# A joint matmul for a group's maxima and the preceding group's sums, and other last loads of w_down, in a decode step of sliding attention beside a gated layer

## The chip, the cores and the metric

The kernel runs on one core of one Trainium2 chip. The metric is device time in microseconds of one launch; a time "of the runs" is the median of several executions. The profile shows one further execution, with its own time. TensorE is the matrix engine (PE in the profile; PEld is its loading of the stationary operand), VectorE is DVE, ScalarE is ACT, GpSimd is POOL, and SyncE (SP) issues nearly all the DMAs.

## The reference

One decode token for B = 2 rows of D = 512. The token is normalised and goes through two parallel branches, whose results are added to it:

```python
xn = _layernorm(x, axis=-1)
# branch A: 32 heads of 128, the last W = 2048 of 8192 cached positions
q = (xn @ wq) as (B, 32, 1, 128)
k, v = k_cache[:, :, Sk - W:, :], v_cache[:, :, Sk - W:, :]
scores = einsum("bhqd,bhkd->bhqk", q, k) * 128 ** -0.5
o = einsum("bhqk,bhkd->bhqd", softmax(scores), v) @ wo
# branch B: F = 1376
h = (xn @ w_gate) * (xn @ w_up)
out = x + o + h @ w_down
```

All is float32. The two caches' windows, wq, wo and the three matrices of branch B are 159 MB, each byte used once.

## The kernel before

**Layout.** All inputs but two small ones lie in one stream in DRAM, in the order in which they are wanted. Of the 128 partitions, 64 hold row b = 0 and 64 hold b = 1. The key window of a head is a tile of 128 x 4096: 32 positions of 128 elements on each partition. The 32 heads form 8 groups of HG = 4, so a group has N = 8 pairs of head and row.

**Loads.** `loads()` (lines 36 to 98) is a plan written out by hand: steps 0 to 24, each one DMA into one of three large buffers (`step0` to `step2`, 128 x 13824) or into the smaller `extra`. A step holds some key tiles `k`, value tiles `v`, and small pieces: four pieces of `wq` for each group, 32 pieces of `wo` (one for each head) and ten pieces of `w_down` (`wd`), each of the last two 128 x 512, which is 256 KB. Step 24 is several loads, each a DMA of its own: v(31), then wd(3, 4, 5), wd(6, 7), wd(8, 9). `issue` puts the loads on SP's queue in this order; a load waits until the old content of its buffer is no longer used.

**Order of the work.** Each engine runs its instructions in the order in which the program names them; `Program.emit` adds a wait where an instruction needs another engine's result. For each step from 3 to 20 (line 510): TensorE weighs the value tiles that have come (`weigh`: 8 matmuls for each head onto a bank of `o_ps`), projects later queries (`project`), multiplies w_down pieces that have come (`down`, onto `acc`); VectorE forms for each key tile the products with the query and their sums (`products`, `sums`, two passes over 128 x 4096). After the fourth head of a group comes `weights(g)` (line 364): VectorE takes the maxima over the free axis, transposes them, reduces again, spreads the result over the columns of `dg` with `mask`, TensorE multiplies the block matrix `halves` with `dg` so that all partitions of a row have the maxima of that row's four heads, VectorE reduces the two columns of each head to `nm` and subtracts it, and ScalarE takes the exponentials, in two halves. The first key tile after that carries `denominators(g)` (line 385): VectorE sums the exponentials over the free axis into `rs`, TensorE multiplies `ones` with `rs` to add up over the partitions; `reciprocals(g)` follows on VectorE. When the fourth value tile of a group has been weighed, `fold` copies the bank to SBUF on ScalarE, `gather` (four matmuls) picks the rows that belong together, `scaled` multiplies with the reciprocals on VectorE and `wo` multiplies the result with a piece of wo onto `acc`, a 2 x 512 accumulator.

**The end** (lines 557 to 590), with g = 7 and its heads 28 to 31: weigh(27) and the fold of group 6, denominators and reciprocals of group 7, gather and scaling of group 6, four wo matmuls onto `acc`, then weigh(28), the accumulator brought into `acc_g`, weigh(29), weigh(30), a fold, gather and scaling of three heads, their wo matmuls, weigh(31), its fold, and the pieces 3 to 9 of w_down around the gather, the scaling and the wo of the last head. In this last stretch the matmuls go onto `acc_g`, which has the 512 output columns as four groups of 128 columns at partitions 0, 32, 64 and 96 (`add_groups`, four matmuls of 128 columns), not onto `acc` (`add_rows`, one matmul of 512 columns). An f32 matmul shows as two passes in the profile.

In the profile nearly all instructions have line 197, which is the helper that emits them; they are told apart by their tiles.

Of the kernel before, what the change touches and what calls it, by code (L numbers as in the profile page):

```python
# [5 lines left out]
ALU = mybir.AluOpType  # L6
AX = mybir.AxisListType
# [3 lines left out]
P = 128  # L11
B, D, H, DH, SK, F = 2, 512, 32, 128, 8192, 1376
W = min(4096, max(256, SK // 4))
HB = P // B
J = W // HB
JG = J // 4
NC = D // P
FB = 4 * P
NFB = -(-F // FB)
# [4 lines left out]
HG = 4  # L24
NG = H // HG
GROUPS = [list(range(g * HG, g * HG + HG)) for g in range(NG)]
N = B * HG
M = 4 * N
CK, CO = J * DH, D
CX = B * NC + 4 * N + 2 * HG + 2 * NFB + 2  # L30
BUFS = 3
WIDTH = 13824
WIDTH_X = 4096
# [2 lines left out]
def loads():  # L36


    def units(kind, *ids):
        w = {"k": CK, "v": CK, "wo": CO, "wd": CO, "wq": HG * DH}[kind]  # L40
        return [(kind, i, w) for i in ids]

    def wq(g, *cs):
        return units("wq", *[(g, c) for c in cs])

    big = {
        1: units("k", 0, 1, 2),
        3: units("k", 3, 4) + units("v", 0),
        4: units("k", 5, 6) + units("v", 1),
        5: units("k", 7, 8) + units("v", 2),  # L50
    }
    k, v = 9, 3
    for n in range(6, 20):
        i = 1 + n % 2
        big[n] = units("k", *range(k, k + i)) + units("v", *range(v, v + 3 - i))
        k, v = k + i, v + 3 - i
    big[20] = units("k", 30, 31) + units("v", 24)
    big[21] = units("v", 25, 26, 27)
    big[22] = units("v", 28, 29)
    small = {  # L60
        1: wq(1, 0, 1, 2),
        3: wq(1, 3) + wq(2, 0, 1),
        4: wq(2, 2, 3) + units("wd", 0),
        5: wq(3, 0, 1, 2),
        6: units("wo", 0, 1, 2),
        7: wq(3, 3) + units("wo", 3) + wq(4, 0),
        8: units("wo", 4, 5, 6),
        9: units("wo", 7) + wq(4, 1, 2),
        10: wq(4, 3) + wq(5, 0, 1),
        11: units("wo", 8, 9, 10),  # L70
        12: units("wo", 11) + wq(5, 2, 3),
        13: wq(6, 0, 1, 2),
        14: units("wo", 12, 13, 14),
        15: units("wo", 15) + wq(6, 3) + wq(7, 0),
        16: units("wo", 16, 17, 18),
        17: units("wo", 19) + wq(7, 1, 2),
        18: wq(7, 3) + units("wd", 1, 2),
        19: units("wo", 20, 21, 22),
        20: units("wo", 23, 24, 25),
        21: units("wo", 26, 27, 28),  # L80
        22: units("wo", 29, 30, 31),
    }
    out = [
        (0, "x", [("c", 0, CX)] + wq(0, 0, 1, 2, 3)),
        (1, 0, big[1] + small[1]),
        (2, 1, [(w, 0, NC * F) for w in ("wg", "wu")]),
        (3, 2, big[3] + small[3]),
    ]
    for n in range(4, 23):
        out += [(n, (1, 0, 2)[(n - 4) % 3], big[n] + small[n])]  # L90
    out += [
        (23, "x", units("v", 30)),
        (24, 0, units("v", 31)),
        (24, 0, units("wd", 3, 4, 5)),
        (24, 0, units("wd", 6, 7)),
        (24, 0, units("wd", 8, 9)),
    ]
    return out
# [136 lines left out]
def build(nc, stream, x_nat, wd_rest, out):  # L235
    pr = Program(nc)
    pe, dve, act, pool = pr.pe, pr.dve, pr.act, pr.pool
# [5 lines left out]
    ones = pr.sb("ones", [P, P])  # L243
# [4 lines left out]
    xc = pr.sb("xc", [P, B, NC])  # L248
    sq = pr.sb("sq", [P, B, NC])
    xn = pr.sb("xn", [P, NC, B])  # L250
    halves = pr.sb("halves", [P, P])
    xnb = pr.sb("xnb", [P, NC, P])
    cst = pr.sb("cst", [P, CX])
    p_all = pr.sb("p", [P, 2, HG, JG, M])
# [1 line left out]
    mt = pr.sb("mt", [P, 32])  # L256
    mtt = pr.sb("mtt", [P, 32])
    mc = pr.sb("mc", [P, 1])
    dg = pr.sb("dg", [P, HG, 2])
    nm = pr.sb("nm", [P, HG])  # L260
    rs = pr.sb("rs", [P, N])
    rec = [pr.sb(f"rec{i}", [P, N]) for i in range(2)]
    oT = [pr.sb(f"oT{i}", [P, N]) for i in range(2)]
    o_sb = [pr.sb(f"o_sb{i}", [P, FB]) for i in range(2)]
# [8 lines left out]
    tr = pr.ps("tr", [P, FB])  # L273
# [28 lines left out]
    dve.memset(zero, 0.0)  # L302
    dve.memset(ones, 1.0)
    dve.memset(mt, 0.0)
    dve.memset(halves, 0.0)
    for b in range(B):
        dve.memset(halves[b * HB : (b + 1) * HB, b * HB : (b + 1) * HB], 1.0)
    for t in gu_ps:
        dve.memset(t, 0.0)
    pool.memset(p_all, 0.0)  # L310
# [1 line left out]
    c0 = got["c", 0]  # L312
    dve.tensor_copy(cst, c0)
    cut = [0]
    for w in (B * NC, 4 * N, 2 * HG, 2 * NFB, 2):
        cut.append(cut[-1] + w)
    xT = cst[:, cut[0] : cut[1]].rearrange("p (b c) -> p b c", b=B)
    pick = cst[:, cut[1] : cut[2]].rearrange("p (r n) -> p r n", r=4)
    mask = cst[:, cut[2] : cut[3]].rearrange("p (n q) -> p n q", q=2)
    sel = cst[:, cut[3] : cut[4]]  # L320
    id2 = cst[:B, cut[4] : cut[5]]

# [37 lines left out]
    def own(ap, counts):  # L360
        steps = (JG * M + 4 * B, 4, M, 1) if len(counts) == 4 else (JG * M + 4 * B, M, 1)
        return bass.AP(ap.tensor, ap.offset, [ap.ap[0]] + [list(t) for t in zip(steps, counts)])

    def weights(g):
        t = s_t[g % 2]
        dve.tensor_reduce(mt[:, 0:HG], t, axis=AX.X, op=ALU.max)
        dve.transpose(mtt, mt)
        dve.tensor_reduce(mc, mtt, axis=AX.X, op=ALU.max)
        dve.tensor_scalar(dg, mask, mc, None, ALU.mult)
        pe.matmul(tr[:, 0 : 2 * HG], halves, dg, start=True, stop=True)  # L370
        dve.tensor_reduce(
            nm, tr[:, 0 : 2 * HG].rearrange("p (n q) -> p n q", q=2), axis=AX.X, op=ALU.max
        )
        dve.tensor_tensor(
            t, t, nm.unsqueeze(2).to_broadcast([P, HG, J]), op=ALU.subtract
        )
        for b in range(B):
            half = slice(b * HB, (b + 1) * HB)
            act.activation(
                own(p_all[half, g % 2, 0, 0, 4 * b : 4 * b + 4], (HG, JG, 4)),  # L380
                t[half].rearrange("p h (i r) -> p h i r", r=4),
                AF.Exp, bias=zero[half], scale=SCALE,
            )

    def denominators(g):
        dve.tensor_reduce(
            rs, own(p_all[:, g % 2, 0, 0, 0:4], (HG, B, JG, 4)), axis=AX.XY, op=ALU.add
        )
        pe.matmul(tr[:, 0:N], ones, rs, start=True, stop=True)

    def reciprocals(g):
        dve.reciprocal(rec[g % 2], tr[:, 0:N])

    def weigh(h, bank=None, first=None, last=None):
        g, hh = divmod(h, HG)
# [22 lines left out]
    def scaled(g, lo=0, hi=N):  # L418
        dve.tensor_tensor(
            oT[g % 2][:, lo:hi], pk_ps[:, lo:hi], rec[g % 2][:, lo:hi], op=ALU.mult  # L420
        )
# [63 lines left out]
    def has(n, kind):  # L485
        return [i for k, i, _ in plan.get(n, []) if k == kind]
# [17 lines left out]
    open_q, open_g, late_wo = [], None, []  # L504
# [5 lines left out]
    for n in range(3, 21):  # L510
        ks, vs = has(n, "k"), has(n, "v")
        for h in late_wo:
            wo(h, add_rows)
        late_wo = []
        full = None
        for h in vs:
            if n > 3:
                weigh(h)
            if h % HG == HG - 1:
                full = h // HG  # L520
                fold(full)
        open_q += [(n, i) for i in has(n, "wq")]
        projections(ks[0] - 1)
        for c in has(n, "wd"):
            down(c, add_rows)
        if full is not None:
            gather(full)
        for x, h in enumerate(ks):
            products(h)
            if open_g is not None:  # L530
                denominators(open_g)
            if n == 3 and x == 0:
                turn()
            projections(h)
            sums(h)
            if open_g is not None:
                reciprocals(open_g)
                open_g = None
            if n == 20 and x == 1:
                weigh(25)  # L540
                weigh(26)
            if h % HG == HG - 1:
                weights(h // HG)
                open_g = h // HG
            if x == 0 and full is not None:
                scaled(full)
                for i in range(full * HG, full * HG + HG):
                    if i in has(n, "wo") or i in has(n - 1, "wo"):
                        wo(i, add_rows)
                    else:  # L550
                        late_wo.append(i)
        if n == 3:
            weigh(vs[0])
        if n < 20:
            issue(min([n] + [m - 1 for m, _ in open_q]) + 3 + (n == 19))

    g = NG - 1
    a, b, c, d = GROUPS[g]
    weigh(a - 1)
    fold(g - 1)  # L560
    denominators(g)
    reciprocals(g)
    gather(g - 1)
    scaled(g - 1)
    for h in GROUPS[g - 1]:
        wo(h, add_rows, last=(h == a - 1))
    issue(99)
# [9 lines left out]
        wo(h, add_groups)  # L577
    weigh(d, bank=0, first=True)
    fold(0)
    for i in range(3, 6):  # L580
        down(i, add_groups)
    gather(0, N - B, N)
    scaled(g, N - B, N)
# [10 lines left out]
def laid_out(x):  # L594
# [3 lines left out]
    a = x["A_x"].reshape(B, D)  # L598
    xs = np.zeros((P, CX), a.dtype)
    xs[:, : B * NC] = a.reshape(B, P, NC).transpose(1, 0, 2).reshape(P, B * NC)  # L600
    o = B * NC
# [3 lines left out]
    o += 4 * N  # L605
    for n in range(HG):
        for q in range(4):
            xs[32 * q + n, o + 2 * n + q % 2] = 1.0
    o += 2 * HG
    for n in range(NFB):  # L610
        for b in range(B):
            xs[32 * n + b, o + n * B + b] = 1.0
# [8 lines left out]
    wo = x["A_wo"].reshape(H, P, D)  # L621
# [4 lines left out]
    wd = x["B_w_down"]  # L626
# [47 lines left out]
```

## Time and profile before

| | us |
|---|---|
| median of 3 runs | 379.8 (379.56 to 380.12) |
| profiled execution | 377.47 |
| its span, first to last instruction | 376.0 |
| VectorE busy | 300.4 |
| TensorE busy | 202.7 |
| ScalarE busy | 15.1 |

The mean granted clock of TensorE is 0.709 of full speed. The profile is that of one execution, whose own time lies 2.3 us under the median of the runs. A group of instructions shows as: engine, operation, out<-in, shapes, count, busy time and mean time of one, and the idle time of the engine just before them with what ended it. The DMA rows give for each shape of load the time from issue to landing, which includes the time it stood in the queue.

### The profile page before, as it was taken

Reading aid. Unit: us, or ns where it says so; the run is one execution under the profiler, and the core shown is the slowest. Engines: PE = TensorE matmul, PEld = TensorE weight load, DVE = VectorE, ACT = ScalarE, POOL = GpSimd, SP = SyncE. Lnnn points to the kernel's source line nnn. Section 1 sums busy time; section 2 is a strip of 40 time slices with the busy share of each in tenths; the row PEclk is TensorE's granted clock in tenths of the full one; section 3 lists DMA queues with packets and bytes.
Section 4 is the critical chain, followed back from the end, with each engine's and each line's share of the span. In section 5 each row is a group of like instructions: output and inputs, shape, how many; then the busy total and the mean of one; then the engine's idle time right before and its main releaser. Section 6 shows DMA issues by size and latency. Waiting matters only on the chain.

```text
span 376.0 us, 2053 instructions
## 1 busy us (share of the span) xinstructions
PE 202.7 (54%) x900; PEld 62.3 (17%) x900; DVE 300.4 (80%) x159; ACT 15.1 (4%) x29; POOL 2.0 (1%) x5
## 2 busy tenths in 40 slices
PE   1552846814574457716457183580665274640996
PEld 1210121200220112101011021110121011200324
DVE  3059979999999997899499499959969995999500
ACT  1000100000000000000100000000000001000101
POOL 2000000000000000000000000000000000000000
PEclk9966856665666856859667756676588585575899
DMA  8999899898998999989999899999999999999995
GB/s 324 471 394 488 376 471 471 372 471 383 465 465 382 461 394 459 465 388 459 394 455 465 388 459 400 453 461 394 453 412 441 465 390 453 423 429 419 440 408 226
DMA packets 4300, 159.67 MB, mean 425 GB/s; under 512 B 482, under 2 KB 610, under 8 KB 1092
## 3 DMA queue, kind: packets, MB, share of 16 engines
q1 hardware_dynamic: 4176, 159.35, 98.4%
q10 hardware_dynamic: 116, 0.20, 0.1%
q8 instruction: 7, 0.11, 0.1%
q14 instruction: 1, 0.01, 0.0%
HBM read 159.48 MB, written 0.07 MB: 424 GB/s over the span
## 4 chain that ended last, share of the span: by engine, by line
DMA 50%; DVE 39%; PE 9%; ACT 0%; issue 0%; SPq 0%
DMA step<-in_stream_dram 50%; DVE s L197 19%; DVE step L197 19%; PE o_ps L197 4%; PE acc L197 3%; PE gu L197 1%; PE q L197 1%; ACT o_sb L197 0%; PE tr L197 0%; SPq L197 0%; DVE rs L197 0%; DVE mt L197 0%; DVE dg L197 0%; DVE mtt L197 0%; DVE mc L197 0%
## 5 line engine op out<-in xcount | busy, mean ns | idle before, releaser
L197 DVE TENSOR_TENSOR step<-step,q 128x4096 f32<-128x4096 f32 x32 | 141.1, 4410 | 41.3 <-DMA step<-in_stream_dram 41.3
L197 DVE TENSOR_REDUCE s<-step 128x32 f32<-128x4096 f32 x32 | 141.4, 4418 | 0.8
L197 PE MATMUL o_ps<-step,p 128*32 128x512 f32 x496 | 90.4, 830 | 60.8 <-DMA step<-in_stream_dram 60.7
L197 PE MATMUL q<-step,xnb 128*128 128x512 f32 x56 | 39.0, 831 | 26.8 <-DVE step L197 19.2
L197 PE MATMUL acc<-step,oT 128*2 128x512 f32 x56 | 38.7, 848 | 26.7 <-DVE oT L197 21.7
L197 PEld LDWEIGHTS o_ps<-step,p 128*32 128x32 f32 x496 | 19.5, 142 | 113.4 <-DMA step<-in_stream_dram 65.4
L197 PEld LDWEIGHTS q<-step,xnb 128*128 128x128 f32 x56 | 12.8, 256 | 51.4 <-DVE step L197 24.8
L197 ACT ACTIVATE p<-s,zero 64x128 f32<-64x128 f32 x16 | 6.4, 399 | 261.5 <-DVE s L197 261.4
L197 PE MATMUL gu<-step,xn 128*2 128x512 f32 (+1 forms) x48 | 9.6, 721 | 7.9 <-DMA step<-in_stream_dram 7.9
L197 PEld LDWEIGHTS acc<-step,oT 128*2 128x2 f32 x56 | 5.0, 102 | 52.9 <-DVE oT L197 22.4
L197 PE MATMUL gu<-cst,o_sb 128*128 128x8 f32 (+2 forms) x72 | 10.3, 270 | 3.9 <-ACT o_sb L197 3.8
L197 PE MATMUL tr<-rs,ones 128*128 128x8 f32 x16 | 3.9, 314 | 15.8 <-DVE rs L197 15.7
L197 PEld LDWEIGHTS gu<-cst,o_sb 128*128 128x128 f32 x72 | 9.5, 206 | 12.3 <-ACT o_sb L197 10.4
L197 DVE TENSOR_TENSOR oT<-gu,rec 128x8 f32<-128x8 f32 (+2 forms) x9 | 1.3, 140 | 12.2 <-PE gu L197 12.2
L197 PE MATMUL tr<-dg,halves 128*128 128x8 f32 x16 | 3.5, 293 | 13.7 <-DVE dg L197 13.7
L197 ACT COPY o_sb<-o_ps 128x512 f32<-128x512 f32 x9 | 5.3, 585 | 54.9 <-PE o_ps L197 54.9
L197 PEld LDWEIGHTS tr<-dg,halves 128*128 128x128 f32 x16 | 2.8, 218 | 22.9 <-DVE dg L197 22.1
L197 PE MATMUL q<-extra,xnb 128*128 128x512 f32 x8 | 5.6, 860 | 1.2 <-DVE xnb L197 1.2
L197 PEld LDWEIGHTS tr<-rs,ones 128*128 128x128 f32 x16 | 3.3, 254 | 16.9 <-DVE rs L197 16.9
L197 DVE TENSOR_REDUCE nm<-tr 128x4 f32<-128x8 f32 x8 | 1.3, 167 | 5.7 <-PE tr L197 5.7
L197 PE MATMUL tr<-st,mean_w 128*128 128x2 f32 x4 | 1.2, 363 | 7.4 <-DVE st L197 7.4
L197 PEld LDWEIGHTS gu<-step,xn 128*2 128x2 f32 x48 | 2.2, 100 | 15.6 <-DMA step<-in_stream_dram 9.1
(50 smaller groups left out, 45.8 us busy)
## 6 DMA issues: line engine op xcount, KB each, us to landing
step<-in_stream_dram SPq DMA_DIRECT2D x20, 6912.0 KB, 31.3
step<-in_stream_dram SPq DMA_DIRECT2D x1, 5504.0 KB, 34.0
step<-in_stream_dram SPq DMA_DIRECT2D x1, 4864.0 KB, 26.1
extra<-in_stream_dram SPq DMA_DIRECT2D x1, 2048.0 KB, 30.7
step<-in_stream_dram SPq DMA_DIRECT2D x1, 2048.0 KB, 27.2
extra<-in_stream_dram SPq DMA_DIRECT2D x1, 1052.0 KB, 5.5
step<-in_stream_dram SPq DMA_DIRECT2D x2, 512.0 KB, 21.5
step<-in_stream_dram SPq DMA_DIRECT2D x1, 768.0 KB, 20.3
```

The costliest lines, as they stand in the source:

```text
L197: ins = getattr(e, method)(*args, **kw)
```

## The change

- `weights(g)`: the matrix `halves` is gone. `mask` and `dg` have four columns for each head instead of two, one for each quarter of the partitions; `dg` and `rs` are two parts of one tile `both` (16 and 8 columns), and one matmul of `ones` with `both` spreads the maxima of group g and adds up the sums of group g - 1. The maxima of a row are then taken from the two columns of that row, with one reduction for each half of the partitions.
- `denominators(g)` forms `rs` alone, without a matmul. `reciprocals(g - 1)` follows `weights(g)` on VectorE, instead of following the sums of the first key tile after `weights(g - 1)`. The last group, which no other follows, has its own matmul with `ones` in the end.
- Loads: wd(3) takes the place of wo(28) in step 21, wo(28) goes to step 22, and the first of the last three loads holds wd(4, 5) alone. The stream is the same but for this order and for 8 more columns of constants.
- `down(3)` goes from the last stretch (onto `acc_g`) to the place between the scaling of group 6 and its four wo matmuls (onto `acc`).

On TensorE the new order between the fold of group 6 and weigh(28) is: the matmul for the last sums, four gather matmuls, down(3), four wo matmuls.

```diff
-CX = B * NC + 4 * N + 2 * HG + 2 * NFB + 2
+CX = B * NC + 4 * N + 4 * HG + 2 * NFB + 2
...
-        21: units("wo", 26, 27, 28),
-        22: units("wo", 29, 30, 31),
+        21: units("wo", 26, 27) + units("wd", 3),
+        22: units("wo", 28, 29, 30, 31),
...
-        (24, 0, units("wd", 3, 4, 5)),
+        (24, 0, units("wd", 4, 5)),
         (24, 0, units("wd", 6, 7)),
         (24, 0, units("wd", 8, 9)),
...
-    dg = pr.sb("dg", [P, HG, 2])
+    both = pr.sb("both", [P, 4 * HG + N])
     nm = pr.sb("nm", [P, HG])
-    rs = pr.sb("rs", [P, N])
...
-    dve.memset(halves, 0.0)
-    for b in range(B):
-        dve.memset(halves[b * HB : (b + 1) * HB, b * HB : (b + 1) * HB], 1.0)
+    dve.memset(both, 0.0)
...
-    mask = cst[:, cut[2] : cut[3]].rearrange("p (n q) -> p n q", q=2)
+    mask = cst[:, cut[2] : cut[3]]
+    dg, rs = both[:, 0 : 4 * HG], both[:, 4 * HG :]
+    top, tot = tr[:, 0 : 4 * HG], tr[:, 4 * HG : 4 * HG + N]
...
         dve.tensor_scalar(dg, mask, mc, None, ALU.mult)
-        pe.matmul(tr[:, 0 : 2 * HG], halves, dg, start=True, stop=True)
-        dve.tensor_reduce(
-            nm, tr[:, 0 : 2 * HG].rearrange("p (n q) -> p n q", q=2), axis=AX.X, op=ALU.max
-        )
+        pe.matmul(tr[:, 0 : 4 * HG + N], ones, both, start=True, stop=True)
+        for b in range(B):
+            half = slice(b * HB, (b + 1) * HB)
+            dve.tensor_reduce(
+                nm[half], top[half].rearrange("p (n q) -> p n q", q=4)[:, :, 2 * b : 2 * b + 2],
+                axis=AX.X, op=ALU.max,
+            )
...
-        pe.matmul(tr[:, 0:N], ones, rs, start=True, stop=True)
 
     def reciprocals(g):
-        dve.reciprocal(rec[g % 2], tr[:, 0:N])
+        dve.reciprocal(rec[g % 2], tot)
...
             if open_g is not None:
                 denominators(open_g)
+                open_g = None
...
-            if open_g is not None:
-                reciprocals(open_g)
-                open_g = None
...
             if h % HG == HG - 1:
                 weights(h // HG)
                 open_g = h // HG
+                if open_g:
+                    reciprocals(open_g - 1)
...
     denominators(g)
+    pe.matmul(tot, ones, rs, start=True, stop=True)
     reciprocals(g)
     gather(g - 1)
     scaled(g - 1)
+    down(3, add_rows)
     for h in GROUPS[g - 1]:
         wo(h, add_rows, last=(h == a - 1))
...
-    for i in range(3, 6):
+    for i in range(4, 6):
         down(i, add_groups)
...
-            xs[32 * q + n, o + 2 * n + q % 2] = 1.0
-    o += 2 * HG
+            xs[32 * q + n, o + 4 * n + q] = 1.0
+    o += 4 * HG
```

More of the change, by code (lines that the diff above doesn't have):

```diff
@@ L250, in build @@
     xn = pr.sb("xn", [P, NC, B])
-    halves = pr.sb("halves", [P, P])
     xnb = pr.sb("xnb", [P, NC, P])
@@ L314, in build @@
     cut = [0]
-    for w in (B * NC, 4 * N, 2 * HG, 2 * NFB, 2):
+    for w in (B * NC, 4 * N, 4 * HG, 2 * NFB, 2):
         cut.append(cut[-1] + w)
```

## The prediction

> **What bounds the kernel now.** I read the page first (shares, queue, chain, groups), then the table by windows, then the chain of waits in order of time for the last 30 us, and the timeline where an edit lands. From the page:
>
> ```profile
> span 376.0 us, 2053 instructions
> ...
> PE 202.7 (54%) x900; PEld 62.3 (17%) x900; DVE 300.4 (80%) x159; ACT 15.1 (4%) x29; POOL 2.0 (1%) x5
> ...
> q1 hardware_dynamic: 4176, 159.35, 98.4%
> ...
> L197 DVE TENSOR_TENSOR step<-step,q 128x4096 f32<-128x4096 f32 x32 | 141.1, 4410 | 41.3 <-DMA step<-in_stream_dram 41.3
> ...
> step<-in_stream_dram SPq DMA_DIRECT2D x20, 6912.0 KB, 31.3
> ```
>
> The load queue is busy for 98.4% of the span with 159.35 MB. VectorE, the busiest engine, has 20% to spare, and its 41.3 us of idle time ahead of the key products is waiting for loads. The windows say the same stage by stage (columns: PE, PEld, DVE, ACT, POOL busy us with counts, granted clock, DMA share, GB/s):
>
> ```profile
> 200.00:300.00 100.00, 52.60 (x212) 15.18 (x216) 84.76 (x38) 2.77 (x6) 0.00 (x0) 0.68 1.00 433
> 300.00:347.60 47.60, 22.58 (x86) 6.04 (x78) 42.60 (x19) 1.38 (x3) 0.00 (x0) 0.64 1.00 433
> ...
> 347.60:351.45 3.85, 3.83 (x20) 0.99 (x24) 3.71 (x5) 0.00 (x0) 0.00 (x0) 0.50 1.12 485
> 351.45:376.00 24.55, 21.03 (x228) 8.93 (x220) 2.64 (x10) 2.55 (x5) 0.00 (x0) 0.99 0.80 335
> ```
>
> Up to 347.6 us the DMA share is 1.00 at 433 GB/s. One load of 6,912 KB (7.08 MB) then takes 16.3 us, and it lands 31.3 us after its issue (median): it stands in the queue for about 15 us before its own bytes move. An engine can be late by several us there and the stream does not notice. So an edit to VectorE or TensorE before 347.6 us is worth nothing while it costs less than that; only the stretch after the landing at 347.57 us can move the end. The chain there:
>
> ```profile
> 308.71 38.86 DMA step<-in_stream_dram
> ...
> 347.62 5.51 PE o_ps L197 x32
> ...
> 353.45 1.90 PE o_ps L197 x16
> ...
> 355.37 0.59 ACT o_sb L197
> ...
> 356.01 1.07 PE gu L197 x8
> ...
> 357.11 0.18 DVE oT L197
> ...
> 357.33 3.17 PE acc L197 x7
> ...
> 362.96 3.62 PE o_ps L197 x32
> ...
> 371.17 0.59 ACT o_sb L197
> ...
> 371.81 1.05 PE gu L197 x8
> 372.87 1.25 PE q L197 x40
> ...
> 374.14 0.29 DVE o_out L197
> ```
>
> From 347.62 to 374.1 us this is TensorE's own order, with three excursions to ScalarE (fold) and VectorE (scaling). No load stands in it. What TensorE gains or loses in this stretch moves the end one for one, unless it then meets a load.
>
> **Part by part.** *Maxima and sums in one matmul.* Ahead of 347.6 us, seven groups lose one matmul and its wait for rs, gain a second nm reduction, and have their reciprocal moved behind the subtraction. All of it lies under a queue 15 us deep: nothing. The same holds for the constants, 4 KB longer, which is 0.01 us at 433 GB/s. Behind 347.6 us lie the last group's steps:
>
> ```profile
> 353.49 0.17 DVE L197 TENSOR_REDUCE nm<-tr 128x4 f32<-128x8 f32 x1 [1.95 <-PE tr L197]
> ...
> 354.01 0.81 ACT L197 ACTIVATE p<-s,zero 64x128 f32<-64x128 f32 x2 [34.78 <-DVE s L197]
> 354.86 0.42 DVE L197 TENSOR_REDUCE rs<-p 128x8 f32<-128x256 f32 x1 [0.88 <-ACT p L197]
> 355.33 0.30 PEld L197 LDWEIGHTS tr<-rs,ones 128*128 128x128 f32 x2 [0.94 <-DVE rs L197]
> 355.33 0.39 PE L197 MATMUL tr<-rs,ones 128*128 128x8 f32 x2
> ```
>
> The group's first matmul stays where it is, between two weighings, and is no cheaper for 24 columns. The second nm costs what the first does, 0.17 us plus a step of 0.03 us, so the exponentials start 0.2 us later. The preceding group's reciprocal (some 0.2 us) runs on VectorE while ScalarE does 0.81 us of exponentials and VectorE waited 0.88 us anyway: hidden, and 0.2 us if that wait were gone. rs then ends near 355.5 instead of 355.28 us, and its matmul, which stays for this group, ends near 355.92 instead of 355.72 us. The gather behind it starts at 356.01 us after the fold, so the 0.2 us is hidden with 0.1 us to spare. I take 0, with 0 to +0.2 as bounds; below nothing is excluded, since the fold waits for the weighing alone.
>
> *One more piece of w_down early.* down(3) leaves the end and becomes one matmul onto acc, placed on TensorE between the gather of group 6 and the four wo matmuls that wait for the scaled oT. The same kind of matmul, down(1) and down(2), stands earlier in the trace at full clock:
>
> ```profile
> 305.71 1.88 PE L197 MATMUL acc<-step,hT 128*2 128x512 f32 x4
> 306.14 0.08 PEld L197 LDWEIGHTS acc<-step,hT 128*2 128x2 f32 x1 [0.35 <-issue]
> ```
>
> Each f32 matmul is two passes (four here for two matmuls), and the second pass starts 0.43 us after the first: 0.86 us for down(3). It starts as the gather drains, at about 357.01 us (the gather ends at 357.08 us in the chain), and frees TensorE at 357.87 us. The wo matmuls started at 357.33 us, so the 0.3 us that TensorE spent waiting for the scaling hides part, and 0.54 us is added to the path. [...]
>
> What it takes away from the end are 8 of 24 short passes behind the last weighing:
>
> ```profile
> 370.83 0.64 PEld L197 LDWEIGHTS q<-step,hT 128*2 128x2 f32 x24 [0.63 <-DMA step<-in_stream_dram]
> 370.92 0.84 PE L197 MATMUL q<-step,hT 128*2 128x128 f32 x24
> ```
>
> The 24 take 0.84 us and end at 371.76 us; the gather behind them starts at 371.81 us because the fold ends at 371.76 us in the chain. With 16 passes TensorE is free 0.28 us earlier and waits for ScalarE instead. Gain: 0 to 0.05 us; I take 0.
>
> *The loads.* wo(28) moves from step 21 to step 22 and wd(3) takes its place, so step 21 keeps its size and lands as before. Step 22 grows by 256 KB, 0.61 us at 433 GB/s, and so do the landings of v(30) and v(31) behind it. The first load of the last three is 256 KB shorter, so from it on all land as before. The count of loads stays. The landings before, from issue and time to landing:
>
> ```profile
> 333.32 0.43 SPq L197 DMA_DIRECT2D extra<-in_stream_dram  x1
> ...
> extra<-in_stream_dram SPq DMA_DIRECT2D x1, 2048.0 KB, 30.7
> ```
>
> ```profile
> 341.73 0.33 SPq L197 DMA_DIRECT2D step<-in_stream_dram  x1
> ...
> step<-in_stream_dram SPq DMA_DIRECT2D x1, 2048.0 KB, 27.2
> ```
>
> ```profile
> 350.88 0.91 SPq L197 DMA_DIRECT2D step<-in_stream_dram  x2
> ...
> step<-in_stream_dram SPq DMA_DIRECT2D x2, 512.0 KB, 21.5
> ```
>
> v(30) lands at 333.32 + 30.7 = 364.0 us, v(31) at 341.73 + 27.2 = 368.9 us, the last piece of w_down near 351.4 + 21.7 = 373.1 us (an estimate: the second issue half-way through the 0.91 us, and a little over the median). TensorE asks for v(30) and v(31) here:
>
> ```profile
> 364.21 0.13 PEld L197 LDWEIGHTS o_ps<-extra,p 128*32 128x32 f32 x4 [0.30 <-DMA extra<-in_stream_dram]
> ...
> 369.10 0.24 PEld L197 LDWEIGHTS o_ps<-step,p 128*32 128x32 f32 x8
> ```
>
> After the change they land at 364.6 and 369.5 us. TensorE, 0.54 us later, asks at 364.75 and 369.64 us: 0.15 and 0.14 us after them, so no wait is added. The two edits lean on each other: were down(3) free, TensorE would ask at 369.10 us and wait 0.4 us for v(31). Either way some 0.4 to 0.5 us comes on top, so I see no way in which this part is free while the end follows TensorE.
>
> *Sum.* 0 + 0.54 - 0 + 0 + 0.01 = +0.55 us; bounds +0.4 (the wait for v(31) alone) to +0.75 (with the 0.2 us of the second nm). The profiled execution took 377.47 us, so 378.0 us for its like. The runs shown have a median of 379.8 us, 2.3 us above that execution; the added time is the same in either, so I forecast 380.4 us, 0.15% more. A measurement of this kernel tells about 0.2% (0.76 us) from no change, so the forecast is mostly "no change", on the slow side.
>
> **The rivals.** *Slower by more: the slacks give way.* Its place is TensorE between 355.3 and 369.7 us. The margins above are 0.1 us (rs matmul before the gather), 0.15 us (v(30)) and 0.14 us (v(31)). If rs comes 0.4 us later instead of 0.2 us, because the reciprocal does not fit beside the exponentials, the gather starts 0.3 us later, and if the loads slip by 0.2 us, v(31) costs another 0.1 us: 0.55 + 0.3 + 0.1 = +0.95 us, 380.8 us. It decides once rs ends after 355.6 us. For it speaks that the second nm sits in the one serial stretch of VectorE that TensorE waits for; against it that VectorE idled 0.88 us right there.
>
> *Hidden: the stream sets the end.* The last piece lands near 373.1 us whatever TensorE does, and eight matmuls and the copy follow. If in ordinary runs the loads end later against TensorE than here by over 1.0 us (that half and the 0.55 us), the added time disappears: +0.0 to +0.1 us, 379.8 us. For it: the last 16 of the chain's final 40 passes start near 373.6 us (24/40 of the 1.25 us after 372.87 us), half a us behind that landing. Against it: the chain holds no load after 347.57 us.
>
> *Faster or slower by the clock.* The windows show TensorE at 0.50 of its clock for 3.85 us after the landing at 347.57 us, then 0.99. Half a clock over 3.85 us costs 1.9 us of the chain. If the changed kernel's runs find the rise earlier against the work than those before do, or later, the end moves: were the slow stretch gone, by -1.9 + 0.55 = -1.35 us, to 378.5 us; were it twice as long, by +1.9 + 0.55 = +2.45 us, to 382.3 us; most runs less. For it: the rise sits in the path. Against it: nothing in the edit touches TensorE's work in the 12 us before 347.57 us, and the runs shown spread over 0.56 us only. [...]
>
> **How the numbers follow.** Forecast, down(3) exposed: 0.52, of which 0.34 within 0.2% and 0.18 above it, since its upper bound touches 0.76 us. Slacks give way: 0.14, slower. Hidden: 0.13, same. Clock: 0.21, of which 0.13 faster and 0.08 slower. Faster 0.13, same 0.47, slower 0.40. The range runs from 379.4 us (hidden, with part of the clock's gain) to 381.2 us (slacks, with part of its loss) and leaves out about 2 in 10. The forecast's own range is 380.2 to 380.6 us.
>
> **What would show it.** Right: in the profile after, an acc matmul from hT with two passes between the gather and the wo matmuls near 357 us, these starting at about 357.9 us; the chain still without a load after 347.6 us and the last copy near 374.7 us; the last gather released by the fold. Slacks: the gather near 356 us released by tr, or the weighing of v(31) by a load. Hidden: the last matmuls released by a load and the copy where it was. Clock: the rise from 0.50 to 1.00 over 1 us away from 351.45 us. Wrong altogether: a DMA share below 1.00 before 347 us, or step 21 landing at another time than 347.6 us.

## Result and profile after

The changed kernel took 378.29 us (median of 6 runs, 378.13 to 378.41), the kernel before 379.68 us beside it (6 runs): ratio 0.9963, 95% interval 0.995 to 0.9976. The forecast was 380.4 us, mostly "no change, on the slow side", with a range from 379.4 to 381.2 us. The measured median is 1.4 us lower than that of before, 0.4%, and lies under the range.

The profile after points the other way. Its execution took 378.41 us, the upper end of its six runs, and that is 0.94 us *more* than the profiled execution of before (377.47 us). From the page, and from the chain of waits in order of time (start us, us, what):

```profile
span 377.1 us, 2019 instructions
...
q1 hardware_dynamic: 4176, 159.35, 98.2%
```

```profile
308.73 38.89 DMA step<-in_stream_dram
...
347.66 5.86 PE o_ps L197 x32
...
353.86 1.90 PE o_ps L197 x16
...
356.41 1.06 PE gu L197 x8
357.47 3.96 PE acc L197 x9
...
363.90 3.62 PE o_ps L197 x32
...
373.80 1.25 PE q L197 x40
...
375.07 0.29 DVE o_out L197
```

Stream, landing of step 21 and order of the tail are as before. The acc piece has nine passes in 3.96 us in place of seven in 3.17 us, and the last copy starts at 375.07 instead of 374.14 us. In the timeline (start us, us, engine, operation):

```profile
355.91 0.39 PE L197 MATMUL tr<-both,ones 128*128 128x8 f32 x2 [0.20 <-DVE both L197]
...
357.40 1.02 PE L197 MATMUL acc<-step,hT 128*2 128x512 f32 x2
...
358.26 3.17 PE L197 MATMUL acc<-step,oT 128*2 128x512 f32 x7
```

From the start of the gather to the first wo matmul it is now 358.26 - 356.41 = 1.85 us; before it was 357.33 - 356.01 = 1.32 us. So down(3) adds 0.53 us, as forecast. The other 0.4 us stand ahead of the gather, where the clock rose later:

```profile
347.62:352.19 4.57, 4.53 (x24) 1.19 (x28) 3.74 (x5) 0.00 (x0) 0.00 (x0) 0.50 1.00 430
```

TensorE ran at half its clock for 4.57 us here and for 3.85 us before; half of the 0.72 us is 0.36 us. By these two profiles the change loses 0.9 us. The question is then not why the changed kernel is ahead, but what the runs of before do that its one profiled execution did not.

### The profile page after: what moved, and what is told of

Its sections match the earlier page's. It is cut to its first block, busy times and chain, and to the rows that moved or that the text cites. A ratio compares the mean times of both kernels' runs of the same rounds, so it can differ in the third digit from the quotient of the medians.

```text
span 377.1 us, 2019 instructions
## 1 busy us (share of the span) xinstructions
PE 202.7 (54%) x880; PEld 59.3 (16%) x880; DVE 302.1 (80%) x165; ACT 15.1 (4%) x29; POOL 2.0 (1%) x5
## 4 chain that ended last, share of the span: by engine, by line
DVE 44%; DMA 42%; PE 11%; issue 1%; another core or an unknown queue 1%; ACT 0%; SPq 0%; DVEq 0%
DMA step<-in_stream_dram 42%; DVE step L197 22%; DVE s L197 20%; PE acc L197 4%; PE o_ps L197 4%; PE q L197 2%; PE gu L197 1%; ACT o_sb L197 0%; PE tr L197 0%; DVE both L197 0%; DVE nm L197 0%; DVE h_sb L197 0%; DVE mt L197 0%; DVE mtt L197 0%
## 5 line engine op out<-in xcount | busy, mean ns | idle before, releaser
L197 PE MATMUL o_ps<-step,p 128*32 128x512 f32 x496 | 89.4, 819 | 71.7 <-DMA step<-in_stream_dram 70.1
L197 PE MATMUL acc<-step,oT 128*2 128x512 f32 x56 | 39.7, 868 | 33.5 <-DVE oT L197 29.2
L197 PE MATMUL q<-step,xnb 128*128 128x512 f32 x56 | 40.6, 863 | 26.5 <-DVE step L197 18.9
L197 PE MATMUL gu<-cst,o_sb 128*128 128x8 f32 (+2 forms) x72 | 9.5, 258 | 3.9 <-ACT o_sb L197 3.8
L197 PE MATMUL tr<-both,ones 128*128 128x24 f32 (+1 forms) x18 | 4.3, 317 | 12.7 <-DVE both L197 12.7
L197 PEld LDWEIGHTS gu<-cst,o_sb 128*128 128x128 f32 x72 | 8.7, 191 | 12.1 <-ACT o_sb L197 10.4
L197 DVE TENSOR_REDUCE nm<-tr 64x4 f32<-64x8 f32 x16 | 2.6, 163 | 6.6 <-PE tr L197 6.5
L197 PEld LDWEIGHTS tr<-both,ones 128*128 128x128 f32 x18 | 3.3, 229 | 23.3 <-DVE both L197 22.5
L197 PE MATMUL gu<-cst,h_sb 128*128 128x6 f32 x8 | 1.9, 362 | 4.4 <-DVE h_sb L197 4.4
```

Source lines behind the costliest of these rows:

```text
L197: ins = getattr(e, method)(*args, **kw)
```

## Experiments

Times are in us; a kernel had 12 runs, beside 35 of before, except where the table says otherwise. The times of every kernel fall either into one group or into two, 2.2 to 2.4 us apart. "Lower" counts the runs in the group of the shorter times; the other is called the upper group below. A "fill" is a matmul whose result nobody reads.

| kernel | median | lowest to highest | lower | median of the lower |
|---|---|---|---|---|
| before (158 runs in all) | 379.44 | 377.18 to 380.19 | 58 of 158 | 377.32 |
| after (18 runs in all) | 378.44 | 377.84 to 380.82 | 14 of 18 | 378.41 |
| joint matmul only | 379.50 | 377.24 to 380.51 | 3 of 12 | 377.55 |
| loads and down(3) only | 378.03 | 377.90 to 380.57 | 10 of 12 | 378.00 |
| after, down(3) late | 379.54 | 377.92 to 380.26 | 5 of 12 | 378.00 |
| before + matmul like down(3) | 378.46 | 377.33 to 380.71 | 7 of 12 | 378.27 |
| before + fill 256 | 377.83 | 377.29 to 378.39 | 12 of 12 | 377.83 |
| before + fill 512 | 377.77 | 377.31 to 378.45 | 12 of 12 | 377.77 |
| after + fill 256 | 378.40 | 377.92 to 378.91 | 12 of 12 | 378.40 |
| joint only + fill 256 | 377.89 | 377.33 to 378.55 | 12 of 12 | 377.89 |

**The kernel before, again** (no edit).

> The kernel before, unchanged, to see an ordinary execution of it: its profiled execution (377.47 us, span 376.0 us) was 2.2 us faster than the median of its six runs (379.68 us), while the changed kernel's own profiled execution (378.41 us) lies inside its runs (378.13 to 378.41 us). Theory A (a DMA engine falls behind: the stream's last loads land later in ordinary executions of before): 379.7 us, and a profile with a span near 378.3 us has the landing of step 21 or of the last pieces some 2 us later than 347.6 and 373.2 us. Theory B (clock): same time, but step 21 lands at 347.6 us and the granted clock rises from 0.50 to 1.00 two to four us later than 351.45 us. Theory C (the profiled execution was an ordinary one and the difference lies outside the span): a span near 376.0 us with a time of 379.7 us.

Measured: 377.56 us median, seven runs at 377.22 to 377.72 us and five at 379.24 to 380.11 us. The profile is of the upper group (379.53 us, span 378.2 us). Step 21 landed at 347.7 us, so theory A falls, and so does C with this span. In the profiles of before and after each value of the granted clock, up to the last, lasts 3.41 us or a multiple of it (before, from 303.66 us on: 6.83, 17.07, 3.41, 3.41, 3.42, 13.65 and 23.89 us); such a piece of 3.41 us is called a stretch here, and the windows of the other profiles are cut likewise. Where the stretches lie against the work differs: TensorE had full clock from 351.45 us on in the first profile of before and from 352.30 us on in this one, though step 21 landed at 347.57 and 347.69 us. In the profiles that show it, of kernels without matmuls ahead of step 21, the 32 weighing passes behind that landing took from 5.10 us (the 256-column fill) to 6.49 us (loads only). The windows of the two profiles of the same kernel, cut at the ends of the stretches (PE, PEld, DVE, ACT, POOL busy us, clock, DMA share, GB/s); first the one that the prediction used:

```profile
365.10:368.52 3.42, 2.49 (x24) 1.19 (x16) 0.17 (x1) 0.58 (x1) 0.00 (x0) 1.00 0.94 398
368.52:371.93 3.41, 3.33 (x65) 1.76 (x66) 0.00 (x0) 0.58 (x1) 0.00 (x0) 1.00 0.88 354
```

then the second, of the upper group:

```profile
347.69:352.30 4.61, 4.56 (x24) 1.19 (x28) 3.83 (x5) 0.00 (x0) 0.00 (x0) 0.50 0.94 405
...
365.96:369.37 3.41, 2.45 (x33) 1.42 (x29) 0.17 (x1) 0.58 (x1) 0.00 (x0) 1.00 0.96 402
369.37:372.78 3.41, 3.41 (x36) 1.33 (x28) 0.00 (x0) 0.00 (x0) 0.00 (x0) 0.50 0.75 303
```

In the second TensorE's clock falls to 0.50 for 3.41 us, from 369.37 to 372.78 us, on top of a later rise (4.61 us at half clock behind the landing in place of 3.85 us, half of which difference is 0.4 us). In its chain the weighing of head 31 takes 3.09 us and the wo matmuls before it 1.20 us; in the first 1.76 and 0.84 us. The first profile, then the second:

```profile
368.55 0.84 PE q L197 x24
369.39 1.76 PE o_ps L197 x16
```

```profile
369.04 1.20 PE q L197 x24
370.23 3.09 PE o_ps L197 x16
```

That is 1.69 us, and with the later rise and landing (0.5 us) the 2.2 us between the groups. Theory B named the clock and the size, but the wrong event: most of the cost is a fall, not a late rise.

**The change in its two parts, and down(3) put back.**

```diff
 joint matmul only: the changed kernel with
-        21: units("wo", 26, 27) + units("wd", 3),
+        21: units("wo", 26, 27, 28),
...
-    down(3, add_rows)
...
 loads only: the kernel before with
+        21: units("wo", 26, 27) + units("wd", 3),
...
+    down(3, add_rows)
...
 down(3) late: the changed kernel with
-    down(3, add_rows)
...
-    for i in range(4, 6):
+    for i in range(3, 6):
```

The first two cuts show only part of each edit: the rest of the load order (step 22, the loads of step 24) and the range of the last pieces of w_down go with it.

> The joint matmul and the moved reciprocals alone; loads and down(3) as in the kernel before. My prediction's terms: 0 against before for the joint matmul. Theory A (fewer TensorE instructions or waits change which DMA engine falls behind): the whole gain is here, and without the 0.54 us of down(3) the time is 377.7 us, 2.0 us under before. Theory B (clock): a gain only if the clock rises earlier here than in before. Rival (the gain is in the loads): 379.7 us, as before.

> The order of the loads and the moved down(3) alone; maxima and sums as in the kernel before. By the prediction's term +0.54 us: 380.2 us. Rival (the gain is in the loads or in the last pieces): 378.3 us, as after. Theory A: the sum of this and of the joint matmul alone, against before, is what the whole change does (-1.4 us).

> The changed kernel with down(3) back among the last pieces (four 128-column matmuls onto acc_g, behind the weighing of head 31); loads as in the changed kernel. The prediction says that TensorE then asks for v(31) 0.54 us earlier, at about 369.1 us of its own trace, but that v(31) lands 0.61 us later than before and makes it wait some 0.4 us: 378.2 us, 0.1 us under after (378.3 us). If v(31) is no limit: 377.75 us, 0.54 us under after. If the clock rise decides, no clear difference.

Measured: the joint matmul alone has the two groups of before (3 of 12 in the lower), the loads with down(3) have 10 of 12 in the lower at 378.0 us, and with down(3) late it is 5 of 12. In the lower group the loads with down(3) cost 0.7 us against before (378.00 to 377.32 us), where 0.54 us was forecast; the median gains 1.4 us only because fewer executions lie in the upper group. So "theory A", a gain in the joint matmul, fails, and "the gain is in the loads" holds for the median and fails for each group. With down(3) late the lower group stays at 378.0 us, not 377.75 us: the order of the loads costs that much by itself. That it does so through the landing of v(31) is inferred, for the one profile of this kernel is of the upper group and has no load in its chain behind step 21.

All three profiles happen to be of the upper group, and all have the fall. The stretch before the fall, and the stretch of the fall, for joint only, loads only, and down(3) late:

```profile
365.45:368.87 3.42, 2.46 (x28) 1.17 (x20) 0.17 (x1) 0.59 (x1) 0.00 (x0) 1.00 0.96 396
368.87:372.28 3.41, 3.41 (x36) 1.58 (x40) 0.00 (x0) 0.00 (x0) 0.00 (x0) 0.50 0.84 338
```

```profile
367.08:370.49 3.41, 2.45 (x36) 1.44 (x32) 0.17 (x1) 0.59 (x1) 0.00 (x0) 1.00 0.97 392
370.49:373.91 3.42, 3.42 (x32) 1.20 (x27) 0.00 (x0) 0.00 (x0) 0.00 (x0) 0.50 0.39 156
```

```profile
366.65:370.06 3.41, 2.45 (x44) 1.63 (x40) 0.17 (x1) 0.59 (x1) 0.00 (x0) 1.00 0.97 396
370.06:373.48 3.42, 3.42 (x28) 0.83 (x20) 0.00 (x0) 0.00 (x0) 0.00 (x0) 0.50 0.54 218
```

Each time TensorE was busy for 2.45 or 2.46 us of the 3.41: the stretch holds the whole wait for the fold of group 7 (0.71 us) and for its scaling (0.26 us). In the lower-group profile of before it was 2.49 us, because the stretch ends inside the second wait, and in that of after 2.67 us, because it ends ahead of the second wait:

```profile
365.85:369.26 3.41, 2.67 (x24) 1.23 (x16) 0.00 (x0) 0.58 (x1) 0.00 (x0) 1.00 0.95 395
```

That gave theory K: the clock falls for one stretch when the stretch before it held too little work, and where the stretches lie against the work differs from execution to execution.

**After again, fillers, and a matmul like down(3).**

```diff
 fill 256 and fill 512: the kernel before with
     fold(g)
+    pe.matmul(
+        q_ps[(NG - 1) % 2][:, 0:256], ones, xnb.rearrange("p c k -> p (c k)")[:, 0:256],
+        start=True, stop=True,
+    )
     gather(g, 0, N - B)
...
 (fill 512: the same with 0:512)
...
 a matmul like down(3): the kernel before with
     scaled(g - 1)
+    pe.matmul(
+        q_ps[(NG - 1) % 2][:B, :], hT[:, 3, 0, :], xnb.rearrange("p c k -> p (c k)"),
+        start=True, stop=True,
+    )
     for h in GROUPS[g - 1]:
```

> The changed kernel again. In the executions so far each kernel falls into two groups, 2.2 us apart: before 377.2 to 377.7 or 379.2 to 380.2 us, the loads alone 377.9 to 378.6 or 380.3 to 380.6 us. The profiles of the slow group show the granted clock at 0.50 for one stretch of 3.4 us near 370 us; those of the quick group don't. Theory K (the clock falls for one stretch where TensorE was idle too long in the stretch before it): the changed kernel has two groups too, near 378.3 and 380.5 us, with nearly all in the first. Rival (the change took time out of the path): one group at 378.3 us, and a quick group of before at 377.4 us is then unexplained.

> The kernel before with one matmul more (ones with 256 columns of the normalised input, into a bank that is not read again), on TensorE between the weighing of head 30 and the gather of group 7, where TensorE waits some 0.7 us for the fold. It adds 0.43 us of TensorE work inside that wait, so nothing to the path. Theory K: busy time in the stretch rises from 2.45 us to some 2.9 us, the clock no longer falls, all executions lie in the quick group: 377.4 us, 2.2 us under before and 0.9 us under after. If only wide, dense matmul time counts and the threshold lies near 1.4 us in the stretch: most but not all executions quick. Rival (the fall of the clock does not hang on this wait): two groups in the shares of before, median 379.6 us.

> The same with 512 columns: 0.85 us of work in a wait of 0.7 us, so some 0.2 us is added to the path. Theory K: all executions in the quick group, 377.5 us. If only dense time counts: more of them quick than with 256 columns. Rival: 379.8 us.

> The kernel before with one matmul more of the shape of down(3) on acc (2 x 512, onto a bank that is not read again), at the place where the changed kernel has down(3). Loads, maxima and sums as before. Theory K in the form that the place of the work against the clock's stretches decides: all behind it comes 0.54 us later, the quick group lies at 377.9 us, and more executions are quick than of before (as with the loads alone, 10 of 12): 378.0 us. Rival (the new loads matter): 380.1 us median, 0.54 us above before, with the shares of before.

Measured: after again has two groups, eight at 377.84 to 378.70 us and four at 380.47 to 380.82 us; its first six runs had none of the second. With either fill all 24 executions lie in the lower group, where before has 58 of 158. One more matmul in a wait of TensorE takes 1.6 us off the median of before; as ratios of the runs beside each other the gain is smaller and not clear of noise (0.9985, 0.9964 to 1.0006, and 0.998, 0.9959 to 1.0002), since executions of before that had no fall gain nothing. The group of the fills reaches from 377.3 to 378.4 us, not to 377.4 us as I wrote: executions with a later rise, which had the fall before, are in it now without it. The 1.4 us in the expectation of the 256-column fill lies between what six profiles without a fill show: the weighing ahead of the wait reached 0.76 to 1.38 us into the stretch before a fall (four profiles), and 1.48 and 1.67 us where none followed (before, after).

This is the test of theory K, and the 24 executions bear it out. The profile of the 256-column fill by itself is no test, since its stretch starts at 364.35 us, ahead of the one from 365.10 us that in the kernel before was followed by no fall. The next experiment gives a pair that is.

The matmul like down(3) does nothing useful and leaves the loads as they were. With it 7 of 12 executions lie in the lower group, at 378.27 us where 377.9 us was forecast; 12 runs alone do not tell that share from 58 of 158. The profiles tell more. Those of after again and of the matmul like down(3) are of the lower group, and their stretches start where kernels without that matmul have the fall:

```profile
365.54:368.96 3.42, 2.71 (x28) 1.21 (x20) 0.00 (x0) 0.59 (x1) 0.00 (x0) 1.00 0.94 393
368.96:372.37 3.41, 3.13 (x58) 1.50 (x57) 0.17 (x1) 0.39 (x1) 0.00 (x0) 1.00 0.82 327
```

```profile
365.68:369.10 3.42, 2.71 (x25) 1.23 (x16) 0.00 (x0) 0.59 (x1) 0.00 (x0) 1.00 0.95 397
369.10:372.51 3.41, 3.15 (x65) 1.65 (x64) 0.17 (x1) 0.47 (x1) 0.00 (x0) 1.00 0.80 324
```

Without a matmul at down(3)'s place, stretches that start at 365.45, 365.96 and 366.65 us were followed by the fall, and only the one from 365.10 us was not. With it those from 365.54, 365.68 and 365.85 us were not, and the one from 367.08 us was.

**The price without the fall.**

```diff
 after + fill 256, joint only + fill 256: the same four lines between
     fold(g)
     gather(g, 0, N - B)
```

> The changed kernel with the 256-column matmul in the wait for the fold of group 7, as in the kernel before with that matmul (377.29 to 378.39 us, one group). Theory K: one group here as well. With the fall of the clock out of both, the change's own price is left: the predicted 0.54 us of down(3), or the 0.61 us by which v(31) lands later, so 377.9 to 379.0 us, median 378.4 us. Rival (the change gains time besides the clock): not above 377.8 us.

> The joint matmul and the moved reciprocals alone, with the 256-column matmul in the same wait. Predicted term: 0 (bound +0.2 us). One group from 377.3 to 378.4 us, median 377.8 us. Rival (the second nm reduction is exposed): 378.0 us.

Measured: 378.40 and 377.89 us against 377.83 us, all 24 executions in one group each. With the fall out of all three, the whole change costs 0.57 us (forecast 0.55) and the joint matmul 0.06 us (forecast 0). Each group spreads over more than 0.9 us, so a difference of two such medians is good to about half a us only.

The profile of joint only with the fill is the pair to that of joint only. Its stretch starts at nearly the same place, 365.59 instead of 365.45 us, and with the fill in it there is no fall behind it:

```profile
365.59:369.00 3.41, 3.08 (x30) 1.48 (x22) 0.17 (x1) 0.59 (x1) 0.00 (x0) 1.00 0.95 392
369.00:372.41 3.41, 3.36 (x66) 1.80 (x66) 0.00 (x0) 0.59 (x1) 0.00 (x0) 1.00 0.84 338
```

**The rise taken out too.** Some TensorE work ahead of the tail, where it waits for step 21:

```diff
 before, after, each with fill 256 and
+                for _ in range(11):
+                    pe.matmul(
+                        q_ps[NG % 2], ones, xnb.rearrange("p c k -> p (c k)"),
+                        start=True, stop=True,
+                    )
                 weigh(25)
```

> The kernel before with the 256-column matmul in the wait, and with eleven matmuls of 128 x 512 on TensorE ahead of the weighing of head 25, where it waits some 12 us for step 21: 22 passes, at 0.43 to 0.85 us some 10.7 to 12.4 us, so that its clock is up when step 21 lands. Theory L (what spreads each group over 1.1 us is when the clock rises after that landing, and the floor of 377.2 us is the landing of v(31)): all executions at 377.2 to 377.4 us. Rival (the floor is TensorE's own work): the 1.9 us of the slow stretch go, 375.7 us or so. Theory K alone says nothing on the spread: 377.8 us.

> The changed kernel with both additions of the kernel before it in this series. Theory L: v(31) lands 0.61 us later, so all executions at 377.8 to 378.0 us, 0.6 us above its counterpart on the kernel before. Rival (down(3) on TensorE is the price, v(31) is not): TensorE is early here, so no difference to the counterpart.

Measured: 377.31 us (377.10 to 378.43) and 377.94 us (377.70 to 379.28; the largest stands alone). Half as forecast: eight of twelve of the first lie at 377.10 to 377.47 us, the others near 378.3 us. The whole change costs 0.63 us here. The chain of the second kernel's profile has no load behind step 21, so this pair does not tell the later v(31) from down(3). In the profile of the first the eleven matmuls ended 2.4 us ahead of the landing of step 21, and the clock fell once more as it landed:

```profile
344.59:348.00 3.41, 0.96 (x6) 0.16 (x8) 3.38 (x2) 0.00 (x0) 0.00 (x0) 1.00 0.90 389
348.00:351.42 3.42, 3.42 (x20) 0.87 (x16) 3.28 (x5) 0.00 (x0) 0.00 (x0) 0.50 1.24 535
```

**Thirteen matmuls, and v(31) earlier.**

```diff
 thirteen: for _ in range(13)
...
 v(31) earlier (before, with thirteen and fill; before, with fill):
-        22: units("wo", 29, 30, 31),
+        22: units("wo", 29, 30),
...
-        (24, 0, units("wd", 3, 4, 5)),
+        (24, 0, units("wd", 3, 4, 5) + units("wo", 31)),
...
 after, with fill: wo(31) from step 22 to the load with wd(4, 5)
```

> The kernel before with the 256-column matmul in the wait and thirteen instead of eleven matmuls ahead of the weighing of head 25; with eleven they ended 2.4 us before step 21 landed, the clock fell once more at 348.0 us, and four of twelve executions lay near 378.3 us. If a shorter wait keeps the clock up: all at 377.1 to 377.3 us. If TensorE's work alone set the end, 1.9 us less: 375.5 us.

> The same with the piece wo(31) moved from step 22 behind v(31), into the load with wd(3, 4, 5), so that v(30) and v(31) land 0.61 us earlier and all else as before. If the landing of v(31) is the floor: 376.6 to 376.8 us, up to 0.6 us below its counterpart, less where the last piece of w_down (landing unchanged at 373.2 us) takes over. If TensorE or the last piece is the floor: no difference.

> The kernel before with the 256-column matmul in the wait, and wo(31) behind v(31), without matmuls ahead of step 21. If v(31) is the floor only of the executions whose clock rises early: the quickest fall from 377.3 to 376.7 us, the slowest stay at 378.4 us, median 377.8 us or a little less. If v(31) binds in all: 377.2 us.

> The changed kernel with the 256-column matmul in the wait, and wo(31) behind v(31), into the load with wd(4, 5): v(30) and v(31) land as in the kernel before, down(3) stays on TensorE's path. If down(3) is the price of the change: 378.4 us median as without the move, the quickest near 377.8 us. If v(31) is: 377.8 us median, as the kernel before with the fill, the quickest at 377.3 us. If v(31) is the floor of early clocks and down(3) the price of late ones: quickest 377.3 us, slowest 378.9 us, median 378.3 us.

Measured: with thirteen matmuls 377.24 us, all twelve between 377.18 and 377.45 us, ratio 0.9953 to before (0.9936 to 0.9971). That is 2.2 us under the runs of before and 1.2 us under those of after, and the spread of the times is gone. In its profile the thirteen ended 2.25 us ahead of the landing, hardly later than the eleven, yet the clock held: they had started 1.4 us earlier, and the stretches lay elsewhere (that of the eleven stands above, that of the thirteen in the last section). So this profile does not show that a shorter wait is what kept the clock up. In its windows the clock is 1.00 from 339.81 to 353.46 us, and then a load stands in the chain:

```profile
341.82 27.18 DMA step<-in_stream_dram
369.01 0.04 issue
369.05 1.92 PE o_ps L197 x16
370.98 0.78 PE q L197 x24
371.76 0.98 PE gu L197 x8
```

The load that lands at 369.0 us is v(31), so with TensorE early the end is set by that landing. With wo(31) behind it the forecast 0.6 us did not come: 377.30 us. The chain shows why:

```profile
350.64 20.23 DMA step<-in_stream_dram
370.88 0.04 issue
370.93 0.84 PE q L197 x24
371.76 0.98 PE gu L197 x8
```

v(31) is out of it, and the next load, with wd(3, 4, 5) and wo(31), lands at 370.88 us, after which the gather starts at the same 371.76 us. The last gather has one floor behind the other. Without the thirteen, 377.75 us against 377.83 us of the fill alone: no clear difference. After, with v(31) back at its old landing: 378.22 us (377.57 to 379.25) against 378.40 us, again no clear difference. Against its own counterpart (377.75 us) it is 0.47 us slower: with v(31) where it was, down(3) on TensorE costs about what the whole change costs. The two prices do not add up.

## Why the prediction was wrong

**The bound.** Right. In the eight profiles whose chain shows it step 21 landed between 347.55 and 347.70 us, with the joint matmul in four of them and without it in four, and the differences arose behind it.

**The joint matmul: 0, bound +0.2 us.** Right as far as the runs tell: 0.06 us between medians, good to about half a us. The profile after shows the place: the matmul for the last sums waited 0.20 us for VectorE and ended at 356.30 us, and the gather started at 356.41 us, right behind the fold, as forecast.

**down(3): +0.54 us.** Right: 0.53 us in the profile. In the three pairs of kernels whose clock has no fall at the end the whole change costs 0.57, 0.63 and, with v(31) where it was, 0.47 us. down(3) started at 357.40 us and the wo matmuls behind it at 358.26 us, so a pass of this f32 matmul of 512 columns took 0.43 us, as in the rows of before.

**The loads: two prices that lean on each other.** Right as a mechanism: the order of the loads alone costs 0.7 us (the lower group with down(3) late), down(3) without the later v(31) 0.47 us, both together 0.57 to 0.63 us, and not their sum. The lowest times go from 377.2 us to 377.7 to 377.9 us in all kernels with v(31) 0.61 us later (an estimate from 256 KB at the 433 GB/s of the windows; from issue to landing it took 28.0 us in the profile after, 27.2 us before), also where down(3) is late. That a TensorE that is early runs into the landing of v(31) shows in the chain of the kernel with thirteen matmuls.

**The sum: this step failed.** It reads: "The runs shown have a median of 379.8 us, 2.3 us above that execution; the added time is the same in either." It is not. The prediction put the difference between the profiled execution and the runs at nothing for the change, without a reason for the 2.3 us. The profiled execution belonged to the lower group of its kernel and the three runs to the upper; what separates the groups is a fall of TensorE's clock near 369 us that costs 1.7 us, and the change alters how often it comes: 58 of 158 runs in the lower group before, 14 of 18 after. So the median jumps from 379.44 to 378.44 us, although each group of after is 1.0 to 1.1 us slower than its counterpart (378.41 to 377.32 us, 380.71 to 379.7 us). That is more than the 0.55 us of the sum, because the groups are not alike: the lower group of after also holds executions with a later rise, as its profile does with 0.36 us, which before would have had the fall.

The means of all runs are 378.84 us before and 378.87 us after: no difference. That the first six runs of before were all of the upper group and the first six of after all of the lower was luck of the draw, and the measured gain of 1.4 us is mostly that. The second comparison of the same pair, 12 runs against 35, gave 1.0017 (0.9991 to 1.0043).

**The clock rival** had the right engine and 0.13 for "faster", but only a rise, earlier or later. That the clock can fall again inside the tail, around waits of 0.71 and 0.26 us, was not in it, nor that the 0.54 us of down(3) would move the work behind it against the stretches. The dense weighing of heads 29 and 30 then reaches further into the stretch, and less of the waits behind it lies in it. In joint only, which has the fall, the weighing ends 1.38 us into the stretch from 365.45 us:

```profile
363.21 3.62 PE o_ps L197 x32
```

In after, which has none, it ends at 367.52 us, 1.67 us into the stretch from 365.85 us. I held against this rival that the runs spread by 0.56 us only; all three lay in one group.

That a matmul at down(3)'s place keeps the clock up more often is shown by the profiles whose stretches start at 365.4 to 366.0 us, two with the fall without it and three without the fall with it, and by the shares: over the three kernels that have it 31 of 42 runs are in the lower group, over the three unfilled ones that do not 66 of 182. That the fall of the clock is what separates the groups is shown by the four profiles of the upper group, which all have it (weighing of head 31 in 2.83 to 3.43 us), by those of the lower that a view shows, which do not (1.72 to 1.92 us in the chains and timelines), and by the fill, which removed the upper group in every kernel that got it.

## What to carry to other kernels

If the profiled execution lies outside the spread of the runs, it is not an ordinary one: look for a second group of times before adding anything to its span, and compare groups with groups. Where TensorE sets the end, look at its short waits in the last stretches of the clock; here a matmul that nobody reads, put into a wait, cost nothing that the runs show and moved the median more (by 1.6 us) than the edit under study (by 1.0 us over all runs). And before a load is put ahead of the last large one, add what comes behind it: here 256 KB are, as an estimate from 433 GB/s, 0.61 us on the landing of v(31), which TensorE waited for in the kernel with thirteen matmuls (to 369.01 us). To move 256 KB behind it gained nothing, since the next load was as late.

## What the runs showed of the hardware

- In the second profile of before TensorE's granted clock fell to 0.50 for one stretch of 3.41 us (from 369.37 us) although no wait of TensorE in the stretch ahead of it was longer than 0.71 us: that stretch had waits of 0.71 and 0.26 us beside a gather of short matmuls (1.06 us), and 2.45 us busy. In joint only a stretch from 365.45 us with 2.46 us busy was followed by half a clock. With the fill in the first wait (0.70 us in the timeline) the stretch from 365.59 us had 3.08 us busy, and 1.00 followed.
- Busy time does not sort the stretches shown. With thirteen matmuls a stretch with 2.23 us busy, all of it 128 x 512 matmuls, was followed by full clock, while 2.45 us with the gather in it was followed by half. With eleven, the stretch from 344.59 us had 0.96 us, and half followed. What decides the clock was not tested. The stretch with the end of the thirteen, and the one behind it:

```profile
343.22:346.64 3.42, 2.23 (x6) 0.69 (x4) 3.39 (x2) 0.00 (x0) 0.00 (x0) 1.00 0.89 384
346.64:350.05 3.41, 2.35 (x24) 0.81 (x28) 3.41 (x1) 0.00 (x0) 0.00 (x0) 1.00 1.19 514
```
